# First tile's attention scores as float32 products of two heads, in the upper and lower halves of the array's rows

## The chip, the cores and the metric

One core of one Trainium2 chip runs the whole program. The metric is the device time of the execution in microseconds (us); lower is better. Before: median 653.32 us of three runs (653.1 to 655.28).

## What is computed

Attention with a top-32 mask over 2 batches, 8 heads, 576 tokens and 64 elements a head, then two feed-forward blocks over the 1152 token rows (512 to 2048 to 512, each with its own activation). All in float32.

```python
scores = scale * np.matmul(q, k.transpose(0, 1, 3, 2))
kth = np.partition(scores, -top_k, axis=-1)[..., -top_k:-top_k + 1]      # top_k = 32
scores = np.where(scores >= kth, scores, -1000000000.0)
attn = exp(scores - max); attn = attn / (sum(attn) + 1e-09)
x = np.matmul(attn, v)                            # rows: 2 x 576, columns: 8 heads x 64
h = x @ w_in;  x = (h * np.tanh(softplus(h))) @ w_out       # block 1
h = x @ w_in2; out = (h * sigmoid(h)) @ w_out2              # block 2
```

## The kernel before

**Tiles.** The 1152 rows are nine tiles of 128 (index `t`), the eight heads four pairs (index `p`). `attention(t, p, rank)` does one tile and one pair: scores into two PSUM buffers `ps_att`, copied to `sc` in halves of 288 keys; four rounds of MAX8 (`m8`) and three of MATCH_REPLACE (`rest`) per head on VectorE find the 32nd largest; exponent (`e`) and mask; nine transposes (L439), the copy `pt`, the product with the values into `ps_misc` (L455, L457), and the product with the turned 1/sum into `xt` (L480). Feed-forward block 1 takes tiles in groups 0; 1; 2; 3,4; 5,6; 7,8, block 2 in groups 0,1; 2; 3,4; 5,6; 7,8.

**Scores.** A key tile comes from HBM as `kraw`, with the 64 rows of each head's keys doubled to 128. It is split: a cast to float32r gives the high part (`kk`, all 128 rows), and a subtraction in the lower 64 rows the low part, so one column of `kk` holds high over low. Queries are split in the same manner into two `qs`, high and low, each doubled over the rows. Two float32r products of 128 rows (L378) then give one head's scores against 288 keys. `load_kv` loads and splits the keys once per batch and pair; tiles 0 to 3 and most of tile 4 use batch 0.

**Buffers.** `kraw` has one buffer, `kk` five, `qraw` and `qs` two each, `wide` (weights as loaded) three, `wraw` (weights in float32) nine.

**Weights.** Weights come from HBM in 8-byte elements, and `convert` turns each of 64 pieces of 128x512 into float32: three steps on ScalarE (L505 twice, L517) and two on GpSimd (L509, L519). Block 1's first group uses the pieces of `w1i` as they come, head pair by head pair (L722).

**Order.** The program is listed by `Plan`. Each step has a rank (a start for its tile from `TILES`, plus a time per pair, or a due time from `DUE1`, `DUE2`), a boost from `OFF` that is taken off the rank, and for each engine that can do it an offset from `FLEX` or `FLEX1`. `emit` goes through modelled time; on each engine the step that can start soonest comes next, and of those that can start at once the one with the lowest rank less boost. Buffers of one kind are given out in the order of their users' ranks (L130, L151 to L156). On the chip each engine and the queue of loads on SP (SyncE) run their list strictly in order.

Of the kernel before, what the change touches and what calls it, by code (L numbers as in the profile page):

```python
# [20 lines left out]
P = 128  # L21
# [7 lines left out]
BLOCK1 = [([0], 'n'), ([1], 'n'), ([2], 'n'), ([3, 4], 'r'), ([5, 6], 'r'), ([7, 8], 'r')]  # L29
BLOCK2 = [([0, 1], 'n'), ([2], 'n'), ([3, 4], 'r'), ([5, 6], 'r'), ([7, 8], 'r')]  # L30

TILES = [(19.37, 6.76), (46.36, 14.1), (106.73, 4.63), (204.37, 9.99), (225.06, 11.69), (258.55, 49.85), (345.98,
         18.22), (519.3, 17.23), (461.45, 16.83)]
DUE1 = [(55.53, 32.57), (72.6, 11.18), (185.18, 33.6), (264.74, 3.6), (326.98, 167.36), (749.26, 11.24)]
DUE2 = [(194.98, 61.15), (262.2, 26.21), (504.62, 78.52), (783.18, 203.62), (946.46, 197.95)]

SBUF_BUFS = dict(kraw=1, kk=5, v=5, qraw=2, qs=2, sc=4, rest=1, e=1, pt=2, m8=10, bias=10, den=8, x=3, dt=2, xt=1,
                 wraw=9, ws=8, hs=2, th=1, wide=3, y=2, o=2)
PSUM_BUFS = dict(att=2, misc=1, h=3, y=2)

FLEX = dict(khi=-199.43, klo=-179.86, qhi=-300.0, qlo=65.82, whi=259.95, wlo=-153.31, ghi=-62.92, glo=163.54,
            hs=286.73, mk=-58.0, se=-300.0, den=105.07, y=271.68, sc=-47.47, pt=57.06, dt=-238.16, xlo=98.83)
FLEX1 = dict(khi=245.84, klo=30.36, qhi=-26.57, qlo=179.72, whi=-172.94, wlo=-208.13, ghi=-191.1, glo=300.0, hs=19.48,
             mk=8.23, se=None, den=-282.09, y=None, sc=252.9, pt=None, dt=239.76, xlo=-232.84)
EARLY = 553.02

OFF = dict(kload=578.07, qload=135.46, k=16.71, q=-13.88, sp=314.62, sc=197.87, bias=39.06, e=246.77, tp=342.92,
           pt=330.03, av=-14.23, x=487.41, den=300.22, dw=35.2, dp=222.21, xt=191.17, m=-75.12, cload=96.71,
           cpn=-97.42, cse=5.37, cw=-99.8, cmid=-37.21, wload=572.6, wsplit=-171.63, wstore=206.7, g=-82.77, hs=-40.2,
           y=-31.25, th=709.1)  # L50

PEEK = 0.05

PORT = 0.34
ADD = 1

HBM = 4
# [13 lines left out]
class Plan:  # L71
# [173 lines left out]
def kernel(ctx: ExitStack, tc, qh, kh, va, w1i, w1o, w2i, w2o, out):  # L245
    nc = tc.nc
    NT, DM = out.shape
    NPAIR, D = qh.shape[1], qh.shape[2] // 2
    S = kh.shape[4]
# [4 lines left out]
    SH = S // 2  # L254
    NB = 2 * NM + 1
# [17 lines left out]
    def get(key, make):  # L273
        if key not in T:
            T[key] = make()
        return T[key]

    def copy_ways(n, get_out, get_in, act=0.0, dve=None, twice=False, psum=False):

        ways = []  # L280
        if act is not None:
            ways.append(("act", act_us(n, psum), act, lambda: nc.scalar.copy(get_out(), get_in())))  # L282
        if dve is not None:
            ways.append(("dve", (dve2_us if twice else dve_us)(n), dve, lambda: nc.vector.tensor_copy(get_out(), get_in()), twice))  # L284
        return ways
# [20 lines left out]
    def load_kv(b, p, rank):  # L306
        if (b, p) in kv_done:
            return
        kv_done.add((b, p))
        kk, vv = ("kk", b, p), ("v", b, p)  # L310
        raw = ("kraw", b, p)
        first = b == 0 and p == 0
        for h in ([0], [1]) if first else ([0, 1],):
            hs = slice(h[0], h[-1] + 1)
            add([("sp", 0.06, 0, lambda hs=hs: nc.sync.dma_start(
                out=get(raw, lambda: sbuf("kraw", [P, 2, S]))[:, hs], in_=kh[b, p][:, hs]))],
                writes=[raw + (i,) for i in h], uses=[(raw, "kraw")], rank=rank - 8, boost="kload", load=len(h) * P * S * 4)
        for h in range(2):
            hi = lambda h=h: get(kk, lambda: sbuf("kk", [P, 2, S], F32R))[:, h]
            lo = lambda h=h: T[kk][D:, h]  # L320
            src = lambda h=h: T[raw][:, h]
            U = [(raw, "kraw"), (kk, "kk")]
            add(copy_ways(S, hi, src, dve="khi", twice=True), reads=[raw + (h,)], writes=[kk + (h, 0)], uses=U,
                rank=rank - 6, boost="k")
            add(tt_ways(S, lo, lambda h=h: T[raw][D:, h], lo, ALU.subtract, dve="klo"), reads=[raw + (h,), kk + (h, 0)], writes=[kk + (h, 1)],
                uses=U, rank=rank - 6, boost="k")
        add([("sp", 0.06, 0, lambda: nc.sync.dma_start(out=get(vv, lambda: sbuf("v", [P, NB + 1, D])), in_=va[b, p]))],
            writes=[vv], uses=[(vv, "v")], rank=rank, load=P * (NB + 1) * D * 4)

    def parts(t):  # L330
        r, res = 0, []
# [11 lines left out]
    def attention(t, p, rank):  # L343
        g, j = group_of[t]
# [3 lines left out]
        pp = parts(t)  # L348
        key = (t, p)
        for b, _, _ in pp:  # L350
            load_kv(b, p, rank)
        K = lambda name, *rest: (name,) + key + rest

        add([("sp", 0.06, 0, lambda: nc.sync.dma_start(out=get(K("qraw"), lambda: sbuf("qraw", [P, 2, P])), in_=qh[t, p]))],
            writes=[K("qraw")], uses=[(K("qraw"), "qraw")], rank=rank - 8, boost="qload", load=P * P * 8)
        for i, (b, r0, r1) in enumerate(pp):
            q = K("qs", i)
            mk = lambda x=slice(0, 2), q=q: get(q, lambda: sbuf("qs", [P, 2, 2, P], F32R))[:, x]
            if len(pp) > 1:
                add([("pool", 0.6, 0, lambda mk=mk: nc.gpsimd.memset(mk().bitcast(F32), 0.0))], writes=[q], uses=[(q, "qs")],  # L360
                    rank=rank - 6)
            raw = lambda r0=r0, r1=r1: T[K("qraw")][:, :, r0:r1]
            hi, lo = (lambda x=x, mk=mk, r0=r0, r1=r1: mk(x)[:, :, r0:r1] for x in range(2))
            U = [(q, "qs"), (K("qraw"), "qraw")]
            add(copy_ways(2 * (r1 - r0), hi, raw, dve="qhi", twice=True), reads=[K("qraw")], writes=[q], uses=U,
                rank=rank - 6, boost="q")
            add(tt_ways(2 * (r1 - r0), lo, raw, hi, ALU.subtract, dve="qlo"), reads=[K("qraw"), q], writes=[q], uses=U,
                rank=rank - 6, boost="q")
        sc = lambda: get(K("sc"), lambda: sbuf("sc", [P, 2, S]))
        for h in range(2):  # L370
            for f in range(2):
# [60 lines left out]
        for c in range(0, NB, 3):  # L432
            tp = K("tp", c)
# [448 lines left out]
```

## Time and profile before

| | |
|---|---|
| median of three runs | 653.32 us |
| profiled execution | 655.83 us, span 654.1 us |
| TensorE busy | 606.1 us (93%) |
| VectorE busy | 539.5 us (82%) |
| ScalarE busy | 476.3 us (73%) |
| GpSimd busy | 382.3 us (58%) |
| mean granted TensorE clock | 0.987 |
| HBM traffic | 271 GB/s over the span |

The profile is of one execution. A share of busy time is a mean over stages with different bounds, so the table of stretches and the chain of waits say more. PE is TensorE's products, PEld its weight loads, DVE is VectorE, ACT ScalarE, POOL GpSimd, SP the queue of loads. L and a number is a line of the kernel before. Casts, copies and subtractions of all kinds share the helper lines L282, L284, L290 and L292; the names of their tiles tell them apart.

### The profile page before, as it was taken

What the parts mean: (1) busy time and instruction counts of PE and PEld (TensorE: products, weight loads), DVE (VectorE), ACT (ScalarE), POOL (GpSimd) and SP (SyncE); (2) the same over time, 40 slices, a digit from 0 to 9 for tenths busy, and PEclk for the clock granted to TensorE, in tenths of its full rate; (3) what the DMA queues carried; (4) which work ended last, traced back from release to release, by engine and by line L of the source; (5) the groups of instructions that cost most, each with busy time, mean ns of one, the idle gap of its engine ahead of it and who ended that gap; (6) DMA issues with size and microseconds to landing.
All of it is one profiled execution on the core that took longest, in us unless ns stands there. A gap on an engine that the chain in (4) does not pass through costs nothing.

```text
span 654.1 us, 13089 instructions
## 1 busy us (share of the span) xinstructions
PE 606.1 (93%) x4536; PEld 537.0 (82%) x4536; DVE 539.5 (82%) x1106; ACT 476.3 (73%) x993; POOL 382.3 (58%) x334
## 2 busy tenths in 40 slices
PE   1298788999999999999999999999999999999997
PEld 1177667999999866668999878999988899999996
DVE  4999999997999999989999979979998234554550
ACT  6799999988699998988978666878777344332321
POOL 6898569761267888987549236556787233322221
PEclk9999967999999999999999999999999999999999
DMA  8987649898789868799999589875876998887752
GB/s 309 293 256 222 197 159 330 312 361 263 204 271 345 276 192 271 268 305 347 389 402 368 151 272 355 316 259 191 272 255 223 374 300 294 278 263 256 246 179 80
DMA packets 85650, 178.34 MB, mean 273 GB/s; under 512 B 8144, under 2 KB 29136, under 8 KB 85584
## 3 DMA queue, kind: packets, MB, share of 16 engines
q1 hardware_dynamic: 85584, 177.50, 80.4%
q8 instruction: 36, 0.59, 0.3%
q14 instruction: 30, 0.25, 0.1%
HBM read 138.94 MB, written 38.54 MB: 271 GB/s over the span
## 4 chain that ended last, share of the span: by engine, by line
PE 53%; DVE 16%; ACT 15%; DMA 7%; issue 4%; POOL 4%; SPq 1%; POOLq 0%; ACTq 0%
PE ps_h L630 20%; PE ps_y L701 12%; PE ps_y L808 11%; DVE m L394 6%; DVE rest L397 5%; ACT ws L505 4%; PE ps_att L378 3%; DMA wraw<-w1i 3%; PE ps_att L439 2%; PE ps_misc L455 2%; ACT wraw L517 2%; ACT pt L282 2%; ACT e L410 2%; DVE e L414 2%; POOL wraw L519 2%
## 5 line engine op out<-in xcount | busy, mean ns | idle before, releaser
L394 DVE MAX8 m<-rest 128x8 f32<-128x576 f32 x216 | 154.4, 745 | 0.1
L397 DVE MATCH_REPLACE8 rest<-m,rest 128x576 f32<-128x576 f32 x144 | 106.2, 741 | 0.0
L509 POOL TENSOR_TENSOR ws<-ws 128x512 int32<-128x512 int32 x64 | 86.7, 1359 | 28.9 <-ACT ws L505 27.2
L378 PE MATMUL ps_att<-kk,qs 128*128 128x288 f32 x320 | 72.8, 346 | 31.6 <-POOL kk L290 24.5
L282 ACT CAST ws<-wraw 128x512 fp32r<-128x512 f32 x93 | 57.4, 621 | 53.8 <-PE ps_h L630 25.3
L519 POOL TENSOR_TENSOR wraw<-wraw,ws 128x512 int32<-128x512 int32 x64 | 85.5, 1346 | 15.9 <-ACT wraw L517 11.0
L505 ACT ACTIVATE ws<-wide,zone 128x512 int32<-128x512 int16 x128 | 94.5, 779 | 0.0
L378 PEld LDWEIGHTS ps_att<-kk,qs 128*128 128x128 f32 x320 | 51.3, 205 | 43.2 <-POOL kk L290 26.0
L292 DVE TENSOR_TENSOR ws<-wraw,ws 128x512 fp32r<-128x512 f32 x65 | 58.9, 924 | 31.3 <-ACT ws L282 30.9
L630 PE MATMUL ps_h<-y,ws 128*128 128x256 f32 x576 | 75.3, 280 | 0.0
L630 PEld LDWEIGHTS ps_h<-y,ws 128*128 128x128 f32 x576 | 73.1, 188 | 2.7
L290 POOL TENSOR_TENSOR ws<-wraw,ws 128x512 fp32r<-128x512 f32 x44 | 57.6, 1318 | 27.3 <-ACT ws L282 14.8
L630 PE MATMUL ps_h<-xt,ws 128*128 128x256 f32 x576 | 72.8, 282 | 0.0
L701 PE MATMUL ps_y<-wide,ws 128*128 128x256 f32 x540 | 71.3, 283 | 0.0
L630 PEld LDWEIGHTS ps_h<-xt,ws 128*128 128x128 f32 x576 | 69.5, 188 | 1.5 <-issue 1.2
L290 POOL TENSOR_TENSOR wide<-th,wide 128x512 fp32r<-128x512 f32 x24 | 31.5, 1313 | 66.7 <-DVE wide L284 65.4
L701 PEld LDWEIGHTS ps_y<-wide,ws 128*128 128x128 f32 x540 | 66.5, 189 | 0.0
L808 PE MATMUL ps_y<-ws,wide 128*128 128x512 f32 x252 | 64.8, 396 | 0.0
L290 POOL TENSOR_TENSOR wide<-hs,wide 128x512 fp32r<-128x512 f32 x24 | 32.0, 1342 | 49.4 <-DVE wide L284 40.2
L439 PE MATMUL ps_att<-ident,e 128*128 128x128 f32 x324 | 52.6, 287 | 6.7 <-DVE e L414 3.9
L701 PE MATMUL ps_y<-hs,wraw 128*128 128x128 f32 x384 | 52.4, 286 | 2.2 <-ACT hs L670 2.2
L394 DVE MAX8 m<-sc 128x8 f32<-128x576 f32 x72 | 52.8, 747 | 1.3 <-ACT sc L282 0.7
(89 smaller groups left out, 1231.5 us busy)
## 6 DMA issues: line engine op xcount, KB each, us to landing
wraw<-w1i SPq DMA_DIRECT2D x64, 256.0 KB, 4.8
wraw<-w2i SPq DMA_DIRECT2D x64, 256.0 KB, 4.0
ws<-w1o_split SPq DMA_DIRECT2D x30, 512.0 KB, 5.1
ws<-w2o_split SPq DMA_DIRECT2D x28, 512.0 KB, 4.4
wraw<-w1o SPq DMA_DIRECT2D x48, 256.0 KB, 5.8
wide<-in_w1i_dram SPq DMA_DIRECT2D x16, 512.0 KB, 5.6
wide<-in_w1o_dram SPq DMA_DIRECT2D x16, 512.0 KB, 5.0
wide<-in_w2i_dram SPq DMA_DIRECT2D x16, 512.0 KB, 5.1
```

What stands on the lines that cost most here:

```text
L282: ways.append(("act", act_us(n, psum), act, lambda: nc.scalar.copy(get_out(), get_in())))
L290: ways.append(("pool", pool_us(n), pool, lambda: nc.gpsimd.tensor_tensor(out=get_out(), in0=get_a(), in1=get_b(), op=op)))
L378: nc.tensor.matmul(o, lhsT=l, rhs=r[:, f * SH:(f + 1) * SH], start=(i == 0), stop=(i == len(ops) - 1))
L394: add([("dve", 0.67, 0, lambda i=i, h=h, src=src: nc.vector.max(out=m8()[:, h, 8 * i:8 * i + 8], in_=src()[:, h]))], reads=srck, writes=[K ...
L397: add([("dve", 0.73, 0, lambda i=i, h=h, src=src: nc.vector.match_replace(out=rest()[:, h], in_to_replace=m8()[:, h, 8 * i:8 * i + 8], in_ ...
L439: nc.tensor.transpose(o[:, i, :], ef[:, (c + i) * P:(c + i + 1) * P], ident)
L505: add([("act", act_us(UNIT) + 0.14, 0, lambda i=i: nc.scalar.activation(pn()[:, i], top(), AF.Relu, scale=ONE16 - 2 * ONE16 * i, bias=zone))],
L509: ways = [("pool", pool_us(UNIT), 0, lambda: nc.gpsimd.tensor_tensor(out=se(), in0=pn()[:, 0], in1=pn()[:, 1], op=ALU.subtract))]
L519: add([("pool", pool_us(UNIT), 0, lambda: nc.gpsimd.tensor_tensor(out=w().bitcast(I32), in0=w().bitcast(I32), in1=se(), op=ALU.add))], rea ...
L630: nc.tensor.matmul(hp[:, c, :], lhsT=l, rhs=rr, start=(i == 0), stop=(i == len(ops) - 1))
L701: nc.tensor.matmul(yp[:, o, :], lhsT=l[:, d * P:(d + 1) * P], rhs=rr[:, c, :], start=(fc == 0 and k == 0 and o == 0), stop=last, skip_grou ...
L808: nc.tensor.matmul(op, lhsT=gg[:, c, i * P:(i + 1) * P], rhs=wt, start=(fc == 0 and k == 0), stop=(fc == NFC - 1 and k == len(ops) - 1))
```

## The change

Tile 0 (`PLAIN = (0,)`) takes keys and queries as they are, without a split. Head 0 is in the upper 64 rows, head 1 in the lower 64, and each half of the keys is one step of two float32 products into two PSUM buffers. The keys' split becomes a function of its own, `split_k`, which is first called by tile 1. Raw and split keys share six buffers of `kk`. All tables of ranks, boosts and offsets have new values.

```diff
-SBUF_BUFS = dict(kraw=1, kk=5, v=5, ...
+SBUF_BUFS = dict(kk=6, v=5, ...
-TILES = [(19.37, 6.76), (46.36, 14.1), (106.73, 4.63), (204.37, 9.99), ...
+TILES = [(28.06, 7.53), (50.67, 14.47), (106.31, 7.12), (204.4, 8.97), ...
-DUE1 = [(55.53, 32.57), (72.6, 11.18), (185.18, 33.6), ...
+DUE1 = [(56.14, 34.7), (72.58, 21.42), (181.07, 37.87), ...
-OFF = dict(kload=578.07, qload=135.46, k=16.71, ... cload=96.71, ...
+OFF = dict(kload=608.39, qload=87.44, k=22.76, ... cload=-16.98, ...
+PLAIN = (0,)
 def load_kv(b, p, rank):
-                out=get(raw, lambda: sbuf("kraw", [P, 2, S]))[:, hs], in_=kh[b, p][:, hs]))],
-                writes=[raw + (i,) for i in h], uses=[(raw, "kraw")], rank=rank - 8, boost="kload", ...
+                out=get(raw, lambda: sbuf("kk", [P, 2, S]))[:, hs], in_=kh[b, p][:, hs]))],
+                writes=[raw + (i,) for i in h], uses=[(raw, "kk")], rank=rank - 8, boost="kload", ...
+def split_k(b, p, rank):          # once per (b, p); the casts and subtractions that stood in load_kv
...
-            U = [(raw, "kraw"), (kk, "kk")]
+            U = [(raw, "kk"), (kk, "kk")]
 def attention(t, p, rank):
             load_kv(b, p, rank)
+            if t not in PLAIN:
+                split_k(b, p, rank)
-        for i, (b, r0, r1) in enumerate(pp):
+        for i, (b, r0, r1) in enumerate(pp if t not in PLAIN else ()):       # query splits
+        for f in range(2) if t in PLAIN else ():
+            sp = [K("sp", h, f) for h in range(2)]
+            def plain(f=f, sp=sp):
+                for h in range(2):
+                    rows = slice(h * D, h * D + D)
+                    nc.tensor.matmul(get(sp[h], lambda: psum("att", [P, SH])), lhsT=T[K("qraw")][rows, h],
+                                     rhs=T["kraw", b, p][rows, h, f * SH:(f + 1) * SH], start=True, stop=True)
+            add([("pe", 0.8, 0, plain)], reads=[K("qraw"), ("kraw", b, p, 0), ("kraw", b, p, 1)], writes=sp, ...
+            for h in range(2):
+                add(copy_ways(SH, lambda h=h, f=f: sc()[:, h, f * SH:(f + 1) * SH], lambda x=sp[h]: T[x], ...
-        for h in range(2):
+        for h in range(2) if t not in PLAIN else ():
             for f in range(2):
                 sp = K("sp", h, f)
```

## Rows read from the trace of the kernel before

**Rows 1.** Stretches: length; PE, PEld, DVE, ACT, POOL busy us; granted clock; DMA share, GB/s
```profile
9.00:60.00 51.00, 29.65 (x171) 24.33 (x172) 50.02 (x105) 45.82 (x94) 43.86 (x36) 1.00 0.90 286
70.00:80.00 10.00, 8.78 (x71) 7.16 (x69) 9.80 (x23) 10.00 (x26) 4.86 (x5) 1.00 0.66 197
80.00:90.00 10.00, 7.36 (x37) 6.10 (x38) 9.72 (x23) 9.97 (x18) 5.26 (x5) 0.58 0.39 113
90.00:100.00 10.00, 7.31 (x43) 6.20 (x43) 10.00 (x23) 9.99 (x22) 6.43 (x7) 0.84 0.59 211
100.00:110.00 10.00, 8.24 (x52) 7.52 (x53) 9.45 (x19) 9.44 (x20) 9.34 (x8) 0.72 0.96 307
110.00:654.00 544.00, 534.47 (x4086) 476.88 (x4084) 440.17 (x896) 377.78 (x792) 298.51 (x259) 1.00 0.81 278
```
**Rows 2.** Chain of waits, 0 to 60 us, then 60 to 104: shares, pieces
```profile
by line: DVE m L394 30.5%; DVE rest L397 23.6%; DMA wide<-in_w1i_dram 10.7%; DVE e L414 8.0%; issue 4.5%; PE ps_h L722 3.4%; ACT ws L505 3.2%; ACT wraw L517 3.2%; ACT pt L282 1.9%; DVE qs L284 1.5%; SPq L354 1.4%; SPq L315 1.3%; ACT e L410 
...
30.42 1.46 DVE rest L397 x2
31.87 1.32 DVE m L394 x2
...
by line: ACT ws L505 26.3%; ACT wraw L517 11.4%; ACT e L410 9.9%; issue 9.1%; ACT pt L282 8.8%; ACT sc L282 7.7%; POOL wraw L519 5.8%; ACT hs L670 4.6%; ACT hs L282 4.3%; POOL ws L509 3.3%; ACT L410 2.9%; ACT dt L282 2.2%; ACT qs L282 2.1%;
```
**Rows 3.** Waits of TensorE, whole span: us in total, times, longest us
```profile
PE ps_att L378 <- POOL kk L290: 24.5, 3, 9.8
```
**Rows 4.** SP queue at the start (start us, us), and stretches of 2 us
```profile
0.72 0.86 SPq L315 DMA_DIRECT2D kraw<-in_kh_dram  x2
1.63 0.90 SPq L354 DMA_DIRECT2D qraw<-in_qh_dram  x2
...
2.00:4.00 2.00, 0.00 (x0) 0.00 (x0) 0.00 (x0) 0.40 (x1) 0.00 (x0) 1.00 0.89 315
6.00:8.00 2.00, 0.47 (x1) 0.14 (x1) 0.00 (x0) 0.40 (x1) 1.92 (x3) 1.00 1.06 358
```
**Rows 5.** Instructions in order of time: start us, us, what, idle time before it
```profile
3.60 1.48 ACT L282 CAST kk<-kraw 128x576 fp32r<-128x576 f32 x2 [1.60 <-DMA kraw<-in_kh_dram]
4.98 0.40 ACT L282 CAST qs<-qraw 128x256 fp32r<-128x256 f32 x1
9.01 0.67 ACT L517 ACTIVATE wraw<-wide 128x512 int32<-128x512 uint32 x1 [2.27 <-DMA wide<-in_w1i_dram]
9.64 0.76 DVE L394 MAX8 m<-sc 128x8 f32<-128x576 f32 x1
31.86 2.73 PE L378 MATMUL ps_att<-kk,qs 128*128 128x288 f32 x8 [8.83 <-POOL kk L290]
34.66 2.81 PE L439 MATMUL ps_att<-ident,e 128*128 128x128 f32 x9
69.20 0.29 DVE L480 TENSOR_TENSOR xt<-ps_misc,dt 128x128 f32<-128x128 f32 x1
```
**Rows 6.** The same view: float32 products at full and half width
```profile
41.41 2.07 PE L722 MATMUL ps_h<-xt,wraw 128*128 128x128 f32 x8 [0.68 <-DVE xt L480]
51.88 1.09 PE L455 MATMUL ps_misc<-pt,v 128*64 128x128 f32 x16
55.42 1.05 PE L722 MATMUL ps_h<-xt,wraw 128*128 128x128 f32 x8
```
**Rows 7.** Groups by line, 0 to 60 us: busy us, mean ns, idle before
```profile
L517 ACT ACTIVATE wraw<-wide 128x512 int32<-128x512 uint32 x15 | 10.1, 676 | 3.6 <-DMA wide<-in_w1i_dram 3.2 <-PE ps_att L439 0.4
L282 ACT CAST qs<-qraw 128x256 fp32r<-128x256 f32 x6 | 2.4, 404 | 1.0 <-DMA qraw<-in_qh_dram 1.0
L290 POOL TENSOR_TENSOR kk<-kraw,kk 64x576 fp32r<-64x576 f32 x8 | 11.6, 1474 | 3.3 <-DMA kraw<-in_kh_dram 3.1
L284 DVE COPY sc<-ps_att 128x288 f32<-128x288 f32 x5 | 2.3, 452 | 8.8 <-PE ps_att L378 8.7
```
**Rows 8.** Waits of TensorE's weight loads, whole span: us in total, times, longest
```profile
PEld ps_misc L455 <- issue: 5.8, 20, 0.8
```

More of the change, by code (lines that the diff above doesn't have):

```diff
@@ L30 @@
 BLOCK2 = [([0, 1], 'n'), ([2], 'n'), ([3, 4], 'r'), ([5, 6], 'r'), ([7, 8], 'r')]
[L32 to L37, printed above, removed]
+TILES = [(28.06, 7.53), (50.67, 14.47), (106.31, 7.12), (204.4, 8.97), (228.13, 9.44), (251.93, 48.93), (339.09,
+         14.84), (544.45, 15.95), (508.61, 11.93)]
@@ L38 @@
+DUE1 = [(56.14, 34.7), (72.58, 21.42), (181.07, 37.87), (264.49, 3.4), (328.08, 127.63), (770.05, 10.76)]
+DUE2 = [(194.96, 63.53), (262.66, 22.33), (489.18, 97.29), (836.89, 208.21), (1017.87, 176.37)]
+SBUF_BUFS = dict(kk=6, v=5, qraw=2, qs=2, sc=4, rest=1, e=1, pt=2, m8=10, bias=10, den=8, x=3, dt=2, xt=1,
                  wraw=9, ws=8, hs=2, th=1, wide=3, y=2, o=2)
 PSUM_BUFS = dict(att=2, misc=1, h=3, y=2)
-FLEX = dict(khi=-199.43, klo=-179.86, qhi=-300.0, qlo=65.82, whi=259.95, wlo=-153.31, ghi=-62.92, glo=163.54,
-            hs=286.73, mk=-58.0, se=-300.0, den=105.07, y=271.68, sc=-47.47, pt=57.06, dt=-238.16, xlo=98.83)
@@ L43 @@
[L43 to L50, printed above, removed]
@@ L52 @@
-PEEK = 0.05
-PORT = 0.34
+FLEX = dict(khi=160.94, klo=-131.85, qhi=-300.0, qlo=-121.8, whi=201.94, wlo=-32.46, ghi=-264.27, glo=-258.34,
+            hs=174.88, mk=151.77, se=-140.65, den=-80.51, y=300.0, sc=-145.93, pt=59.31, dt=-5.98, xlo=175.24)
+FLEX1 = dict(khi=141.86, klo=136.65, qhi=-26.45, qlo=133.59, whi=145.08, wlo=-291.44, ghi=-103.6, glo=-11.08,
+             hs=38.75, mk=39.78, se=None, den=-118.72, y=None, sc=296.41, pt=None, dt=300.0, xlo=-49.66)
+EARLY = 559.36
+OFF = dict(kload=608.39, qload=87.44, k=22.76, q=-16.29, sp=238.91, sc=165.63, bias=127.91, e=228.22, tp=367.53,
+           pt=451.83, av=14.38, x=624.87, den=370.98, dw=96.55, dp=228.54, xt=170.88, m=-115.49, cload=-16.98,
+           cpn=-115.59, cse=25.73, cw=-53.73, cmid=-26.87, wload=612.68, wsplit=-319.71, wstore=228.61, g=-104.3,
+           hs=-21.89, y=26.54, th=732.7)
@@ L55 @@
+PEEK = 0.03
+PORT = 0.21
 ADD = 1
@@ L315, in load_kv @@
             add([("sp", 0.06, 0, lambda hs=hs: nc.sync.dma_start(
-                out=get(raw, lambda: sbuf("kraw", [P, 2, S]))[:, hs], in_=kh[b, p][:, hs]))],
-                writes=[raw + (i,) for i in h], uses=[(raw, "kraw")], rank=rank - 8, boost="kload", load=len(h) * P * S * 4)
+                out=get(raw, lambda: sbuf("kk", [P, 2, S]))[:, hs], in_=kh[b, p][:, hs]))],
+                writes=[raw + (i,) for i in h], uses=[(raw, "kk")], rank=rank - 8, boost="kload", load=len(h) * P * S * 4)
+        add([("sp", 0.06, 0, lambda: nc.sync.dma_start(out=get(vv, lambda: sbuf("v", [P, NB + 1, D])), in_=va[b, p]))],
+            writes=[vv], uses=[(vv, "v")], rank=rank, load=P * (NB + 1) * D * 4)
+    kk_done = set()
+    def split_k(b, p, rank):
+        if (b, p) in kk_done:
+            return
+        kk_done.add((b, p))
+        kk, raw = ("kk", b, p), ("kraw", b, p)
         for h in range(2):
@@ L326, in load_kv @@
                 uses=U, rank=rank - 6, boost="k")
-        add([("sp", 0.06, 0, lambda: nc.sync.dma_start(out=get(vv, lambda: sbuf("v", [P, NB + 1, D])), in_=va[b, p]))],
-            writes=[vv], uses=[(vv, "v")], rank=rank, load=P * (NB + 1) * D * 4)
     def parts(t):
@@ L369, in attention @@
         sc = lambda: get(K("sc"), lambda: sbuf("sc", [P, 2, S]))
-        for h in range(2):
+        for f in range(2) if t in PLAIN else ():
[5 more added lines that the diff above has]
+                                     rhs=T["kraw", b, p][rows, h, f * SH:(f + 1) * SH], start=True, stop=True)
+            (b, _, _), = pp
+            add([("pe", 0.8, 0, plain)], reads=[K("qraw"), ("kraw", b, p, 0), ("kraw", b, p, 1)], writes=sp, rank=rank - 10,
+                boost="sp", uses=[(x, "ps_att") for x in sp] + [(K("qraw"), "qraw"), (("kraw", b, p), "kk")])
+            for h in range(2):
+                add(copy_ways(SH, lambda h=h, f=f: sc()[:, h, f * SH:(f + 1) * SH], lambda x=sp[h]: T[x], dve="sc", psum=True),
+                    reads=[sp[h]], writes=[K("sc", h, f)], uses=[(sp[h], "ps_att"), (K("sc"), "sc")], rank=rank - 10, boost="sc")
+        for h in range(2) if t not in PLAIN else ():
             for f in range(2):
```

## Prediction

> **What bounds the kernel now.** I read the table of stretches first. From 110 us to the end TensorE is busy 534.5 of 544.0 us, so there only its work and the moment at which it is fully supplied count; ahead of that it is not the bound [rows 1]. The chain of waits says what is: up to 60 us over half of it is VectorE's top-32 search (MAX8 30.5%, MATCH_REPLACE 23.6%), and from 60 to 104 us it is ScalarE, mostly turning weights into float32 (26.3% and 11.4%) [rows 2]. The reader should see in the table that both are full there: ScalarE has 5.2 us idle between 9 and 60 us and none from 70 to 80, VectorE 1.0 us and 0.2. In 70 to 110 us TensorE loses time in two ways: 8.3 us idle, and a granted clock of 0.58, 0.84 and 0.72 (1.00 is the 2.4 GHz level, 0.50 the 1.2 GHz level) in three stretches, which on 7.36, 7.31 and 8.24 us of work is 3.1 + 1.2 + 2.3 = 6.6 us. Together 14.9 us that an earlier supply could give back [rows 1]. Last come the waits of TensorE's queue: 24.5 us, in three waits, for GpSimd's key splits [rows 3]. That is the stall which the change takes away. TensorE has little else to do early, but its queue is in order: the third pair's scores wait 8.8 us and start at 31.86 us, and the transposes of pair 0 stand behind them, at 34.66 [rows 5].
>
> **The change, part by part.** All sums are against the profiled execution, 655.83 us (span 654.1 and 1.7 around it), which lies 2.5 above the median of 653.32; differences carry over to the median.
>
> *Order of the loads.* Raw keys had one buffer; now they share six with the split ones, and nothing holds them at the start. SP takes its steps by rank less boost. For keys that is 28.06 - 8 - 608.39 = -588 for pair 0, and -566 for pair 3; for the first queries 28.06 - 8 - 87.44 = -67; for the first weights 16.1 - 10 + 17.0 = +23. So all four pairs' keys (288 + 288 + 3 x 576 KB) now go ahead of the first queries, where before only pair 0's did [rows 4]. Three more transfers of 576 KB are 1.77 MB, at 0.36 MB per us (358 GB/s in a full stretch [rows 4]) 4.9 us. To the first queries there are 2.49 MB: counted from 2.0 us that is 6.9 us, and 0.7 us go from the last byte to use (pair 0's first half, 0.29 MB, counted in the same way at 315 GB/s, is there at 2.9 us, and its cast starts at 3.60 [rows 4, 5]): usable at 9.6 us against 4.98 before [rows 5]. The same 4.9 us go on the first weights, used at 9.01 us before [rows 5]. SP issues seven transfers in 3.2 us at 0.45 each, so the issue itself is no bound.
>
> *The products.* A float32 product is two records. Eight records of 128 columns take 2.07 us early and 1.05 us later [rows 6]; for 288 columns, and two heads (four records), that is 2.3 or 1.2 us one after the other. No row shows two halves of rows side by side. The nearest are the value products, which use two halves of the columns: 16 records in 1.09 us, where 8 at full width take 1.05, a ratio of 0.52 [rows 6]. From the two ends, side by side (0.52) and in turn (1.0), I take the first: 1.2 us at the early pace. There are two PSUM buffers, so the second half of the keys waits until the first is copied (0.45 us [rows 7]). First search with both heads at hand: 9.6 + 1.2 + 0.45 + 1.2 + 0.45 = 12.9 us. Before, VectorE searched without gap from 12.48 us and had 1.6 us of it done by then (MAX8 at 9.64, one replacement [rows 5]): an effective start of 10.9. Loss +2.0; in turn it is 2 x 1.1 more, of which the first head's lead hides about 1, so +3.2. In sum TensorE spends 8 x 1.2 = 10 us on these scores against 4 x 2.73 = 11 before [rows 5], where it has 21 of 51 us free [rows 1]: nothing.
>
> *A rule that speaks against it.* TensorE's weight loads of the value products, the first to use half the columns after full-width work, start 0.29 us late (5.8 us in 20), put down to nothing but issue [rows 8]. The Trainium skill (TensorEngine Tiling, Key Properties) says that changing the tiling mode drains TensorE, which agrees with that row; the row halves of this change would pay it too. By it two changes stand before the first search, about 0.6 us, and the sum below would end 0.6 later; without it, as below.
>
> *Splits removed and moved.* Tile 0's query splits go: one on VectorE (1.5% of 60 us on the chain, 0.9 [rows 2]), the others on ScalarE at 0.40 each [rows 7], of which I count one behind 9 us. VectorE's side: +2.0 - 0.9 = +1.1. The key splits (0.74 a head on ScalarE [rows 5], 1.47 on GpSimd [rows 7]) aren't removed: tile 1 needs them. Pair 0's casts, which lay in ScalarE's empty first 9 us, now come behind. ScalarE: +4.9 + 1.5 - 0.4, less what it fills of its 5.2 us idle: between +0.8 and +6.0. Of the idle 3.2 us are waits for these weights [rows 7]; since the later key loads leave the queue I take them as filled, with 0.8 us of the other waits: +2.0. The two engines run beside each other: the worse counts, +2.0. GpSimd is given 11.6 us of room [rows 7], and has 5 us idle in each of the stretches from 70 to 90 us [rows 1], which hide its later splits; without that cover 2 x 1.47 us a pair would show.
>
> *What the freed queue gives.* With no product of tile 0 waiting for a split, pair 0's transposes follow its mask, and pair 3's scores can be ready at any time. Tile 0's fourth and last x lands at 69.20 us [rows 5]. VectorE needs per pair about 8 x 0.66 + 6 x 0.73 + 1.6 + 0.6 = 11.9 us (two searches 1.32, two replacements 1.46, the mask 8.0% of 60 us in three pairs [rows 2], and 0.6 for the small ones), 47 for the tile, of the 56.7 between 12.48 and 69.20: some 9 us of it went to tile 1. Tile 0's last x can come between 0 and 9 us earlier. I take half, 4.5: the first block's hidden layer ends that much sooner, and out of the 14.9 us lost in 70 to 110 so much comes back. What is late next is ScalarE's conversion of w1o, since it is full at 70 to 100 us [rows 1].
>
> *Ranks.* They move every later step; the profile can't show the new order. TensorE's idle time behind 110 us is 9.5 us, so little can be gained there; a worse order could open gaps as well. I take zero, with -3 and +3 as bounds, a third of that idle time.
>
> **Sum:** +2.0 - 4.5 = -2.5, so 653.3 for such an execution and 650.8 for the median. Bounds of the terms: +0.8 - 9 = -8.2 and +6.0 - 0 = +6.0; with ranks 642 to 662.
>
> **The rivals.**
> 1. *ScalarE keeps the gain.* It is full from 70 to 100 us whatever arrives; an earlier x of tile 0 then only makes its conversions the wait. For: nothing of its work there goes. Against: its 5.2 us idle earlier can take some. The -4.5 shrinks to about -2: 653.3.
> 2. *The keys in front decide (slower).* Place: the SP queue's first seven loads. Price: the 4.9 us of three key transfers on weights and queries. It decides if ScalarE can't fill its gaps and tile 0's order stays as it was: then +3 to +6 reach TensorE's full stretch, which has 9.5 us in 544 to take them back. For: VectorE is at 98% from 9 us on, ScalarE at 90% and from 70 us at 100% [rows 1]. Against: VectorE's own loss is only 1.1. Middle +4: 657.3.
> 3. *The heads don't run side by side.* The change then isn't what it says; the start is 1.2 later, 652.0.
> 4. *The new order gains behind 110 us too:* 3 more on top of a gain of 4, 646.
>
> **How the numbers follow.** Chances: forecast 0.38 (own range 648 to 651.3), first rival 0.20, second 0.32, third 0.05, fourth 0.05. A measurement of this kernel tells 0.3%, 2.0 us, from no change: faster is below 651.4, slower above 655.3. Faster: 0.38 + 0.05 = 0.43; same 0.20 + 0.05 = 0.25; slower 0.32. The range that leaves out 2 in 10: 643 to 660.
>
> **What would show it.** Right: the first MAX8 at about 12 to 13 us (9.64 before), the first weights used near 14; no wait of TensorE's scores for a GpSimd key split before 46 us; tile 0's fourth x before 66 us; stretches 80 to 110 with a granted clock nearer 1. The pair of heads: starts of upper and lower rows a few tens of ns apart for side by side. Wrong: the full stretch of TensorE starting after 110 us (rival 2), or ScalarE full and x early but nothing gained (rival 1). A first MAX8 before 10 us would say that the queue of loads was misread.

## The result and the profile after

The changed kernel takes 661.89 us in the median of four runs (660.86 to 663.78); the kernel before took 653.49 in four beside it. The ratio is 1.0126, 95% interval 1.0094 to 1.0159: slower by 8.4 us, where 2.5 us faster was forecast, and outside the range. The profiled execution after took 660.86 us (span 658.0), the one before 655.83 (span 654.1). So the two traces hold 5.0 us of the 8.4, 3.9 of them in the span: the execution traced before was one of the longer ones (the spans of its 91 runs beside the experiments have a median of 652.4), the one after the shortest of four.

The stretches of the changed kernel, with the columns of [rows 1]:

```profile
9.00:60.00 51.00, 35.54 (x208) 25.22 (x209) 45.38 (x98) 45.16 (x98) 41.02 (x32) 0.97 0.85 269
60.00:70.00 10.00, 4.97 (x29) 4.17 (x27) 10.00 (x20) 8.68 (x17) 9.69 (x8) 0.76 0.79 246
70.00:80.00 10.00, 8.51 (x42) 6.67 (x41) 10.00 (x23) 9.21 (x21) 7.53 (x8) 0.50 0.74 239
80.00:90.00 10.00, 7.40 (x57) 6.90 (x56) 8.97 (x20) 8.91 (x19) 6.38 (x6) 0.84 0.70 220
90.00:100.00 10.00, 7.63 (x52) 6.74 (x51) 9.73 (x24) 9.96 (x18) 5.95 (x6) 0.70 0.53 173
100.00:110.00 10.00, 8.43 (x75) 7.38 (x73) 9.96 (x23) 10.00 (x24) 7.33 (x7) 1.00 0.78 240
110.00:658.00 548.00, 535.99 (x4088) 477.17 (x4087) 445.79 (x921) 379.50 (x795) 268.95 (x238) 1.00 0.80 276
```

The reader should see two things. TensorE did more between 9 and 60 us than before (35.5 us against 29.7 [rows 1]), as the change means it to. VectorE did less: 45.4 us against 50.0, and it is this third busy column that most of the rest is about. The prediction counted 14.9 us of TensorE's time lost from 70 to 110 us, part of which was to come back. The same sum from these rows is 8.0 us idle and 7.7 for the granted clock (0.50, 0.84, 0.70 and 1.00 on 8.51, 7.40, 7.63 and 8.43 us of work), 15.8 in all: none of it came back.

The same view for VectorE alone, over 0 to 110 us and from there to the end of its last MAX8; first the kernel before, then the changed one:

```profile
0.00:110.00 110.00, 99.32 (x211) 0.92 0.78 247
110.00:503.30 393.30, 375.21 (x802) 1.00 0.84 287
```
```profile
0.00:110.00 110.00, 94.05 (x203) 0.88 0.78 247
110.00:506.80 396.80, 376.92 (x802) 1.00 0.83 285
```

And single instructions of the changed kernel (start us, us, what, idle time before it), which answer to [rows 4, 5]: loads, first products, first weights, first search; then tile 0's fourth x, what TensorE waited for ahead of it, and two key splits.

```profile
0.72 2.29 SPq L317 DMA_DIRECT2D kk<-in_kh_dram  x5
3.05 1.15 SPq L367 DMA_DIRECT2D qraw<-in_qh_dram  x2
4.24 4.54 SPq L526 DMA_DIRECT2D wide<-in_w1i_dram  x3
11.76 1.33 PE L389 MATMUL ps_att<-kk,qraw 64*128 64x288 f32 x4 [11.76 <-DMA qraw<-in_qh_dram]
13.53 0.66 ACT L544 ACTIVATE wraw<-wide 128x512 int32<-128x512 uint32 x1
15.64 1.41 DVE L421 MAX8 m<-sc 128x8 f32<-128x576 f32 x2
9.08 2.75 POOL L292 TENSOR_TENSOR kk<-kk 64x576 fp32r<-64x576 f32 x2 [1.92 <-ACT kk L284]
23.77 2.80 POOL L292 TENSOR_TENSOR kk<-kk 64x576 fp32r<-64x576 f32 x2
66.02 2.08 PE L749 MATMUL ps_y<-xt,wraw 128*128 128x128 f32 x8 [4.45 <-POOL wraw L546]
76.87 0.28 DVE L507 TENSOR_TENSOR xt<-ps_misc,dt 128x128 f32<-128x128 f32 x1
```

The first search starts at 15.64 us, 6.0 later than before. TensorE's 24.5 us of waits for key splits [rows 3] are gone from its list, but it is idle for 37.5 of the first 110 us, where it was idle for 38.4 before. The waits have other names now; these are the longest:

```profile
PE ps_att L389 <- DMA qraw<-in_qh_dram: 11.8, 1, 11.8
PE ps_att L466 <- DVE e L441: 8.2, 11, 2.6
PE ps_att L466 <- ACT sc L284: 5.2, 5, 3.3
```

**A distance that stays the same.** The last MAX8, VectorE's last search, ends at 503.3 us before and at 506.8 after; the span ends 150.8 and 151.3 us behind it. In the fifteen traces of the changed kernel and of the experiments below that distance is 150.6 to 151.5 us, while the end itself moves over 17.6 us. (In the rows below a MAX8 that starts at 519.13 us and takes 0.75 is such a last search.) So what makes one version slower than another lies ahead of the last search. The distance doesn't say which engine it is, for two of them are nearly full up to there. All engines from 320 to 503 us, before and after:

```profile
320.00:503.00 183.00, 181.87 (x1466) 165.00 (x1465) 173.97 (x372) 137.80 (x315) 111.64 (x96) 1.00 0.82 283
320.00:503.00 183.00, 182.16 (x1480) 165.99 (x1479) 171.90 (x367) 141.19 (x316) 113.72 (x96) 1.00 0.83 291
```

TensorE is idle for 1.1 and 0.8 us there, VectorE for 9.0 and 11.1. In all sixteen traces TensorE loses at most 1.1 us from 320 us to the last search, so the versions part earlier. The table gives VectorE's idle time and work up to its last search, which add up to where that search ends, and TensorE's idle time from 110 us to the end of the span:

| kernel | VectorE idle 0 to 110 | VectorE idle behind 110 | VectorE work | last MAX8 ends | span | TensorE idle behind 110 |
|---|---|---|---|---|---|---|
| before | 10.7 | 18.1 | 474.5 | 503.3 | 654.1 | 9.6 |
| after | 16.0 | 19.9 | 471.0 | 506.8 | 658.0 | 12.0 |
| late start | 14.7 | 18.7 | 473.8 | 507.2 | 657.7 | 11.2 |
| twice the products | 12.3 | 16.9 | 474.2 | 503.3 | 653.9 | 9.8 |
| more work for VectorE | 9.7 | 17.3 | 480.0 | 507.0 | 657.8 | 10.9 |
| den ahead | 13.5 | 19.8 | 472.7 | 506.0 | 657.4 | 13.2 |
| late splits | 17.2 | 21.6 | 471.8 | 510.6 | 661.9 | 13.8 |
| copies on ScalarE | 10.5 | 19.3 | 473.9 | 503.7 | 654.5 | 10.4 |
| relief | 10.7 | 18.1 | 473.6 | 502.3 | 653.1 | 9.9 |
| old products, new order | 27.0 | 20.0 | 472.9 | 519.9 | 671.0 | 13.5 |
| the same, early queries | 20.2 | 20.2 | 472.6 | 512.9 | 664.2 | 13.5 |

VectorE's columns are read as the two pairs above: length less busy. Each row is one execution, and executions of one kernel lie 2 to 6 us apart (653.10 to 655.28 before), so smaller differences between rows show nothing by themselves. Idle time and work add up to the end for any engine; the sum alone names no cause.

Two things can be read. The change gives VectorE 5.3 us more idle time ahead of 110 us and 1.8 behind, and takes 3.5 us of work off it. That work is not just tile 0's: up to the last search VectorE even has six score copies more than before (25 against 19), and the new tables give other steps to other engines, among them nine casts of weights (2 against 11) and five subtractions for split x (9 against 14). And the last column parts the two orders. In the eight traces with the changed kernel's order it is 12.0 to 13.8 us, in the eight with the order before 9.5 to 11.4; the means are 2.8 us apart, and the gaps lie between 110 and 320 us.

### The profile page after: what moved, and what is told of

Read it like the earlier page. It is cut to its first block, busy times and chain, and to the rows that moved or that the text cites. A ratio compares the mean times of both kernels' runs of the same rounds, so it can differ in the third digit from the quotient of the medians.

```text
span 658.0 us, 13060 instructions
## 1 busy us (share of the span) xinstructions
PE 608.5 (92%) x4536; PEld 534.2 (81%) x4536; DVE 539.8 (82%) x1123; ACT 474.7 (72%) x989; POOL 350.3 (53%) x311
## 4 chain that ended last, share of the span: by engine, by line
PE 56%; DVE 29%; ACT 10%; DMA 2%; issue 2%; SPq 0%; DVEq 0%; ACTq 0%
PE ps_h L657 23%; DVE m L421 12%; PE ps_y L835 11%; PE ps_y L728 10%; DVE rest L424 10%; DVE e L441 4%; PE ps_misc L482 3%; ACT ws L532 3%; PE ps_att L405 3%; PE ps_att L466 2%; ACT sc L284 1%; DMA qraw<-in_qh_dram 1%; PE ps_misc L484 1%; ACT pt L284 1%; ACT wraw L544 1%
## 5 line engine op out<-in xcount | busy, mean ns | idle before, releaser
L284 ACT CAST ws<-wraw 128x512 fp32r<-128x512 f32 x101 | 61.1, 621 | 51.1 <-PE ps_h L657 26.8
L546 POOL TENSOR_TENSOR wraw<-wraw,ws 128x512 int32<-128x512 int32 x64 | 83.8, 1324 | 7.6 <-ACT wraw L544 6.5
L292 POOL TENSOR_TENSOR ws<-wraw,ws 128x512 fp32r<-128x512 f32 x49 | 64.0, 1327 | 16.7 <-ACT ws L284 12.3
L294 DVE TENSOR_TENSOR ws<-wraw,ws 128x512 fp32r<-128x512 f32 x60 | 45.2, 758 | 30.9 <-ACT ws L284 30.6
L466 PE MATMUL ps_att<-ident,e 128*128 128x128 f32 x324 | 55.1, 295 | 14.9 <-DVE e L441 8.2
L405 PE MATMUL ps_att<-kk,qs 128*128 128x288 f32 x288 | 61.3, 329 | 3.0 <-ACT sc L284 1.6
L466 PEld LDWEIGHTS ps_att<-ident,e 128*128 128x128 f32 x324 | 39.7, 149 | 27.4 <-issue 9.6
L284 ACT COPY pt<-ps_att 128x384 f32<-128x384 f32 x107 | 47.7, 479 | 7.5 <-PE ps_att L466 7.1
L424 DVE MATCH_REPLACE8 rest<-m,sc 128x576 f32<-128x576 f32 x72 | 53.1, 740 | 0.0
```

The source lines that it names most:

```text
L292: ways.append(("pool", pool_us(n), pool, lambda: nc.gpsimd.tensor_tensor(out=get_out(), in0=get_a(), in1=get_b(), op=op)))
L405: nc.tensor.matmul(o, lhsT=l, rhs=r[:, f * SH:(f + 1) * SH], start=(i == 0), stop=(i == len(ops) - 1))
L424: add([("dve", 0.73, 0, lambda i=i, h=h, src=src: nc.vector.match_replace(out=rest()[:, h], in_to_replace=m8()[:, h, 8 * i:8 * i + 8], in_ ...
L466: nc.tensor.transpose(o[:, i, :], ef[:, (c + i) * P:(c + i + 1) * P], ident)
L546: add([("pool", pool_us(UNIT), 0, lambda: nc.gpsimd.tensor_tensor(out=w().bitcast(I32), in0=w().bitcast(I32), in1=se(), op=ALU.add))], rea ...
```

## The experiments

Theories: T, the prediction's own, by which TensorE's early waits are worth time; A, the late start; B, the new form of the products costs by itself; C, the new order costs; D, formed after the first seven runs, that VectorE's chain sets the end and all else counts by what it does to that. Ratios are to the kernel before, run on the same chip; they compare means, so a difference of two medians can be 1 us off them. Where an order is edited, all other steps keep engine and place.

**Queries first**, in the changed kernel's order:

```diff
-SP: keys of pairs 0, 1, 2, 3; queries of pairs 0, 1; w1i
+SP: keys of pair 0; queries of pairs 0, 1; keys of pairs 1, 2, 3; w1i
-ScalarE, GpSimd: key splits of pair 1 ahead of the first score copy
+ScalarE, GpSimd: key splits of pair 1 behind it
```


> The changed kernel with its order of steps kept, except that the first two query loads go ahead of the keys of pairs 1 to 3, and pair 1's key splits go behind the first copy of scores. Theory A, the late queries: VectorE's search starts near 9 us instead of 15.6, and since VectorE is full to 140 us the total falls by 3 to 5 us from 661.9, to 657 to 659. Theory B, the late weights: they land as late as in the changed kernel, so the total stays within 1.5 us of 661.9. Theory C, the new order of the later steps: nothing at the start matters, within 1.5 us too.

Measured: 660.01 us, ratio 1.0078 (1.0055 to 1.0100). The first search starts at 10.4 us in place of 15.6, and only 1.9 us of the 8.4 come back by the medians, 3.1 by the ratios (the intervals of the two just overlap): VectorE then waits 4.2 us for two `den` steps that stand in ScalarE's queue behind conversions. The time lies between A's 657 to 659 and the 660.4 or more of B and C.

**Start as before**: in addition the first three `w1i` loads ahead of the keys of pairs 1 to 3, and pair 1's splits behind the first conversion.

```diff
-SP: ...; keys of pairs 1, 2, 3; w1i, three loads
+SP: ...; w1i, three loads; keys of pairs 1, 2, 3
```


> The same, with the first three weight loads too ahead of the keys of pairs 1 to 3, so that the first loads go in the order of the kernel before. Theory A: like the run with the queries first, 657 to 659. Theory B: weights 4.5 us earlier, ScalarE and GpSimd convert them earlier, and the total falls by 4 us or more more than with the queries alone, to 653 to 657. Theory C: within 1.5 us of 661.9.

Measured: 661.14 us, 1.0090 (1.0065 to 1.0115). Weights are used from 8.6 us on, and nothing is gained by it, as C said.

**Late start**: the kernel before, with three more loads of 576 KB ahead of its first queries.

```diff
 keys of pair 0, second half: nc.sync.dma_start(out=kraw, in_=kh[b, p])
+for i in range(3): nc.sync.dma_start(out=unused, in_=kh[0, i + 1])
```


> The kernel before, in its own order, with three more loads of 576 KB (keys of pairs 1 to 3, into buffers that are not yet in use, read by nobody) ahead of its first queries and weights. Theories A and B: the start is as late as in the changed kernel, queries near 11 us and weights near 13, and 4 to 8 us of it reach the end: 657 to 661. Theory C: the later order is that of the kernel before and takes the delay up in its gaps, below 655.

Measured: 658.40 us, 1.0059 (1.0037 to 1.0082). The first search starts at 13.95 us, 4.3 later, and the end of the trace comes 3.6 later. In the old order a late start is passed on nearly whole, as A and B said.

**Same rows**: the changed kernel with both heads in the upper 64 rows (keys and queries lie in both halves, so the scores are the same).

```diff
-rows = slice(h * D, h * D + D)
+rows = slice(0, D)
```


> The changed kernel with both heads' products in the upper 64 rows of the array (the keys and queries lie in both halves, so the result is the same), nothing else moved. If heads in two halves of the rows run side by side, four records take about 2.3 us early instead of 1.33, VectorE starts 1 to 2 us later, and the total rises by 1 to 2 us. If they don't, nothing changes, within 1 us.

Measured: 664.97 us, 1.0164 (1.0135 to 1.0194). TensorE's products of two pairs, in the changed kernel and here:

```profile
35.00 0.76 PE L389 MATMUL ps_att<-kk,qraw 64*128 64x288 f32 x4
38.23 0.76 PE L389 MATMUL ps_att<-kk,qraw 64*128 64x288 f32 x4
```
```profile
35.22 1.24 PE L389 MATMUL ps_att<-kk,qraw 64*128 64x288 f32 x4
38.42 1.23 PE L389 MATMUL ps_att<-kk,qraw 64*128 64x288 f32 x4
```

Two heads in two halves of the rows take 0.76 us, in one half 1.24 (granted clock 1.00 in both): they do run side by side, at 0.61 of the time. Read one by one, the records of the two heads start 0.006 or 0.007 us apart at 35.00 and again at 35.35 in the changed kernel; here the four start at 35.22, 35.57, 35.81 and 36.05. The total is 3.1 us above the changed kernel's, but the two intervals overlap.

**Old order**: the new products in the order of the kernel before.

```diff
-tile 0: query splits; eight steps of split products, one copy behind each
+tile 0: per half of the keys one step of two plain products, a copy on VectorE and one on ScalarE
-SP: queries of four later pairs where they stood
+SP: each behind the plain products that free its buffer
```


> The new products of tile 0 (float32, two heads in the two halves of the rows, key tile shared) in the order of emission of the kernel before: the twelve split products and query splits of tile 0 are left out, the eight plain products stand where each pair's first split product stood, and four query loads go behind the plain products that free their buffers. Every other step keeps its engine and its place. Theory C (the new order costs, the product form does not): the wait for key splits (24.5 us of TensorE's idle time by 42 us, rows 3) goes, the end follows by at most a few us: 648 to 654, not slower than before. Theory B (the new form itself costs, by row halves, by keys held longer or by copies): slower than before, 656 to 662, near the changed kernel.

Measured: 658.39 us, 1.0048 (1.0032 to 1.0064): 3 us slower than before, with no wait for a key split left. That is B's range, and C's forecast (not slower) fails. TensorE's waits did not go, they changed their names, and it is idle for 40.4 of the first 110 us:

```profile
PE ps_att L507 <- DMA qraw<-in_qh_dram: 6.1, 1, 6.1
PE ps_att L507 <- DMA kk<-in_kh_dram: 5.8, 1, 5.8
PE ps_att L507 <- ACT sc L402: 5.4, 3, 4.2
PE ps_att L507 <- DVE rest L542: 4.7, 1, 4.7
```

VectorE had eight score copies here in place of five, and 1.4 us waits for the second half of the keys, since both PSUM buffers are taken by the first.

**Old products**: the mirror, split products and query splits at the plain ones' places in the changed kernel's order.

> The mirror: the split products and query splits of tile 0 as before, put at the places of the plain ones in the order of emission of the changed kernel; its loads, ranks, conversions and shared key buffers are kept. Theory C: the order decides, so 660 to 666, as slow as the changed kernel or slower by the 2 to 4 us that the splits cost in the first 40 us. Theory B: the product form decides, so near before: 652 to 657.

Measured: 674.57 us, 1.0303 (1.0275 to 1.0331), which neither theory gave. The first row is of TensorE's waits up to 60 us, the second VectorE's last search:

```profile
PE ps_att L524 <- ACT qs L403: 21.0, 3, 12.0
...
519.13 0.75 DVE L540 MAX8 m<-rest 128x8 f32<-128x576 f32 x1
```

The edit had put the query casts where they held TensorE up for 21 us, so the run measured itself more than the order. It is repeated better below.

**Late splits**: queries first, and each key split behind the conversions that stand ahead of its first reader.

```diff
-ScalarE, GpSimd: key splits of pairs 0 to 3 within the first 27 us; batch 1's pair 0 from 57 us
+ScalarE, GpSimd: each shortly before tile 1's scores of the pair; batch 1's pair 0 near its old place
```


> The changed kernel with the queries ahead of the keys of pairs 1 to 3 (as in the run queries first), and with every key split moved behind the weight conversions that stand ahead of its first reader: pairs 0 to 3 shortly before tile 1's scores of that pair, batch 1's pair 0 near the place it had before. Nothing else moves. If the early splits are what holds the first MLP layer back (they stand ahead of the conversions for which TensorE waited 4.4 us at 61.6 us in the changed kernel): the fourth x of tile 0 and the first h come earlier, 654 to 657. If not, 659 to 661 as the run with queries first (660.0).

Measured: 663.63 us, 1.0124 (1.0098 to 1.0149), a miss: slower than queries first, not faster. VectorE's waits up to 110 us:

```profile
DVE sc L296 <- PE ps_att L399: 8.2, 2, 6.8
DVE den L503 <- ACT den L499: 5.0, 3, 4.3
DVE m L431 <- ACT sc L294: 2.0, 1, 2.0
```

With conversions in the splits' place, ScalarE's small steps for the search stand behind conversions that wait for their loads. So no gain from later splits was found, though the edit brought waits of its own. These seven traces laid beside each other gave D; the next two runs test it on the kernel before.

**Twice the products**:

```diff
-for i, (l, r) in enumerate(ops):
+for i, (l, r) in list(enumerate(ops)) * (2 if t == 0 and p > 0 else 1):
```


> The kernel before with the split products of tile 0's pairs 1 to 3 issued twice into the same tiles, which adds about 8 us of TensorE work in the first 42 us (three times 2.73, rows 5) and makes the scores of three pairs 2.7 us later. Theory D (VectorE's chain of MAX8 and MATCH_REPLACE8 is what the first 110 us wait for, and it runs with hardly a gap behind 12.5 us; TensorE's waits for key splits lie beside it): no change, 653 to 656. Theory T, the prediction's own (TensorE's waits on the way to the first scores are on the path): 657 to 663.

Measured: 656.00 us, 1.0018 (1.0005 to 1.0032). TensorE's products of pairs 1 and 2 (before: 20.31 and 31.86, 2.73 us each), and VectorE's last search:

```profile
20.81 3.67 PE L378 MATMUL ps_att<-kk,qs 128*128 128x288 f32 x16 [10.20 <-POOL kk L290]
33.01 4.21 PE L378 MATMUL ps_att<-kk,qs 128*128 128x288 f32 x16 [8.53 <-POOL kk L290]
...
502.52 0.76 DVE L394 MAX8 m<-rest 128x8 f32<-128x576 f32 x1
```

The edit added less than meant, since the longer blocks ran faster (0.23 and 0.26 us a product, not 0.34): the scores are complete 1.4 and 2.6 us later. By the ratio the time rises by 1.2 us (0.3 to 2.1), and VectorE is idle for 1.6 us more ahead of 110 us. The last search ends where it did in the trace before, which was one of the longer executions. Both waits for key splits are still there, 18.7 us long.

**More work for VectorE**:

```diff
-nc.vector.max(out=m8[...], in_=src)
+[nc.vector.max(out=m8[...], in_=src) for _ in range(2 if t == 0 and p == 1 else 1)]
```


> The kernel before with the eight MAX8 of tile 0's second pair done twice, which adds 8 x 0.67 = 5.3 us of VectorE work at 24 to 36 us and nothing to any other engine. Theory D: the end moves by most of it, 658 to 660. Theory T: VectorE has room in the stretch in which TensorE waits, 654 to 656.

Measured: 661.18 us, 1.0108 (1.0083 to 1.0133): 7.1 us (5.4 to 8.7) for 5.3 us of work. The last search, in the shortest of the six runs (659.59 us):

```profile
506.27 0.76 DVE L394 MAX8 m<-rest 128x8 f32<-128x576 f32 x1
```

The second run is clear: T forecast 654 to 656 for it, and VectorE's early work is paid in full. The first fits D, but with half the delay that was meant it is weaker evidence against T: products that come up to 2.6 us later cost 1.2, about what VectorE's idle time grew by. Both edits lie ahead of 42 us, so they say nothing of what sets the pace behind 110.

**Den ahead**: queries first, and ScalarE's `den` of tile 0's pairs 0 and 1 ahead of the conversions that VectorE had waited behind.

```diff
-ScalarE: ws, ws, den (pair 0), ...; sc, sc, qs, den (pair 1)
+ScalarE: den (pair 0), ..., ws, ws; den (pair 1), sc, sc, qs
```


> The changed kernel with the queries first (660.0 us) and, besides, ScalarE's two small den steps of tile 0's first two pairs ahead of the conversions and casts behind which VectorE waited 2.3 and 1.9 us for them. Everything else of the new order stays, the w1i conversions become 1.4 us later. Theory D: VectorE gets back some 4 us of its first 110, so 655 to 657. Theory C (the new order of conversions and splits costs by itself): no better than 660, up to 662.

Measured: 660.62 us, 1.0085 (1.0066 to 1.0105): no gain, a miss for D's number. VectorE, stretches and waits up to 110 us:

```profile
0.00:110.00 110.00, 96.50 (x206) 0.92 0.79 251
110.00:506.00 396.00, 376.17 (x798) 1.00 0.83 285
```
```profile
DVE sc L296 <- PE ps_att L399: 9.4, 3, 6.6
DVE xt L517 <- PE ps_misc L494: 1.9, 2, 1.1
DVE den L503 <- ACT den L499: 1.2, 2, 0.9
```

The 3 us taken from `den` came back as other waits but for 1.3 us. The distance to the end stays (506.0 + 151.4), but D's estimate of what one wait is worth fails: behind it stands the next.

**Copies on ScalarE**: the old order with the new products, VectorE relieved.

```diff
-pairs 1 to 3: of four score copies two on VectorE
+pairs 1 to 3: all four on ScalarE
+pair 0: ScalarE's copies ahead of its first conversions
```


> The new products in the old order again (658.4), with VectorE relieved: the score copies of pairs 1 to 3 all on ScalarE (VectorE does two copies in place of eight, 6 x 0.45 = 2.7 us less), and pair 0's copies ahead of ScalarE's first weight conversions, so that no copy waits behind them. Theory D: 2.5 to 5 us less than that run, 652 to 656, at or under the kernel before. Theory B (the new form costs by itself): 657 to 659.

Measured: 656.31 us, 1.0029 (1.0017 to 1.0041), by the ratios 1.2 us less than the old order with eight copies (2.1 by the medians; the intervals overlap), still 1.9 above the kernel before, and between D's range and B's. VectorE starts at 8.52 us and has as little idle time ahead of 110 us as before. Where its lead goes is seen at 300 us:

```profile
302.40 0.62 ACT L402 CAST ws<-wraw 128x512 fp32r<-128x512 f32 x1 [3.14 <-DMA wraw<-w1i]
302.93 0.39 ACT L402 COPY sc<-ps_att 128x288 f32<-128x288 f32 x1
```
```profile
303.35 0.76 DVE L539 MAX8 m<-sc 128x8 f32<-128x576 f32 x1 [2.04 <-ACT sc L402]
```

ScalarE waits 3.1 us for a weight load, a score copy stands behind it, and VectorE waits 2.0 us for the copy.

**Copy ahead**: the last kernel with that copy ahead of the waiting split, and `den` ahead of conversions. The recorded text speaks of the first pair's `den`; the edit moves that of all four pairs of tile 0.

```diff
-ScalarE: ws (w1i, waits for its load); sc (tile 6, pair 0)
+ScalarE: sc (tile 6, pair 0); ws (w1i, waits for its load)
-ScalarE: conversions (w1i); den (tile 0, each pair)
+ScalarE: den (tile 0, each pair); conversions (w1i)
```


> The last run (new products, old order, copies on ScalarE, 656.3 us) with two steps of ScalarE's queue exchanged with their neighbours: the score copy of tile 6's first pair ahead of the split of a w1i chunk that waited 3.1 us for its DMA at 299 us (VectorE waited 2.0 us there for that copy), and den of tile 0's first pair ahead of one weight conversion (VectorE waited 1.1 us at 22.6 us). Theory D (each us of VectorE's waits before its last MAX8 moves the end): 1.5 to 2.5 us less, 653.5 to 655, level with the kernel before. If VectorE's waits are not what is left there: 656 as before.

Measured: 657.82 us, 1.0050 (1.0033 to 1.0068), a miss: the 2.0 us wait is gone, 1.7 us of others stand near it, and ahead of 110 us VectorE is busy 1.1 us less.

**Relief**: the kernel before, with two score copies and a query cast of tile 0 on ScalarE.

```diff
-VectorE: sc (pair 1), sc (pair 2), qs (pair 2)
+ScalarE: sc (pair 1), sc (pair 2), qs (pair 2)
```


> The kernel before, in its own order, with three VectorE steps of tile 0 given to ScalarE at the same place: one score copy each of pairs 1 and 2 (0.45 us) and the query cast of pair 2 (0.88 us), together 1.8 us less VectorE work before 36 us. Theory D: the end comes earlier by up to that, 652 to 653.5 (ratio 0.997 to 0.999), less what waits for ScalarE take back. Theory T: no change, 654 to 655.

Measured: 654.93 us, 1.0004 (0.9990 to 1.0018): no change; the 1.8 us that D allowed at most lie outside the interval. Added VectorE work is paid in full, work taken away gives nothing that can be measured, so D as it was put (all counts by VectorE's chain) is not borne out. Why is not settled. The wait at 300 us in the run with the copies on ScalarE, for a load that comes no earlier, is one place where a lead can end; TensorE, nearly full from 110 us on, is a rival that no run tests.

**Old products, early queries**: the second mirror.

```diff
-ScalarE, GpSimd: query splits directly ahead of their pair's products
+ScalarE, GpSimd: pairs 0 and 1 behind the key splits of pair 1, pairs 2 and 3 well ahead of their products
```


> As the run with the old split products in the changed kernel's order (674.6 us), but with tile 0's query splits early in place of directly ahead of their products: pairs 0 and 1 behind the key splits of pair 1, pairs 2 and 3 two thirds of the way from their loads to their products. In that run TensorE waited 21.0 us for ScalarE's query casts, so it told little of the order. Here key and query splits are both ahead of the products, and products, copies, loads and conversions stand in the changed kernel's order. Theory C (the order costs, the product form little): 660 to 665. If the product form is worth much in this order: 666 or more. If the new form itself is what costs: 655 to 658.

Measured: 665.86 us, 1.0200 (1.0170 to 1.0231). TensorE still waited 15.7 us for query casts, 12.3 of them at the very start, where the changed kernel waits 11.8 for the loads. So in the new order the old form is slower than the new one, with those waits in it, and the old order with the old form faster than all. For the old form the order's cost can't be told from the waits. With the new form it is the step from 1.0029 (copies on ScalarE) to 1.0126, 0.0097 of 654 us or 6.3, of which queries first gave 1.9 to 3.1 back.

No version beat the kernel before.

## Why the prediction was wrong

- **What bounds it, and what the freed queue gives.** The chain and the table were read rightly for VectorE (98% busy between 9 and 60 us [rows 1, 2]), and then TensorE's 24.5 us of waits [rows 3] were called the stall that the change takes away, and its going the source of the term -4.5. That step failed. VectorE had hardly any room for earlier scores, and TensorE's waits passed to loads, copies and VectorE's own steps: idle 38.4 of the first 110 us before, 37.5 after, 40.4 with the new products in the old order. Tile 0's fourth x was to come 4.5 us earlier, before 66 us; it came at 76.87, 7.7 later than [rows 5]. The first three came about 5 us earlier (35.9, 48.9 and 57.8 against 41.1, 53.8 and 61.7): with VectorE full, tiles 0 and 1 shared it otherwise. At 66.02 TensorE had waited 4.45 us for a weight converted late. The new products in the old order were 3 us slower, not faster.
- **Behind 110 us** only TensorE's work and its supply were to count. From 320 us on the rows agree (0.8 to 1.1 us idle to the last search). Between 110 and 320 TensorE is idle for 4.7 us before and 7.5 after.
- **Order of the loads.** Right in kind, too small. The queries were usable at 11.76 us, not at 9.6. The sum counted the keys in front at 358 GB/s; between 4 and 8 us 309 and 293 were reached, and the three weight loads issued behind the queries moved at the same time (by 11 us some 3.0 MB had come, not 2.49). The weights came as said (13.53 against about 14).
- **Start of the search.** Taken as 10.9 to 12.9 us, +2.0; it was 15.64, +4.7. Of the 2.7 us more, 2.2 are the queries, the rest the second half of the products (1.43 us behind the copies). The late start in the old order shows its worth, 3.9 us; in the new order restoring it gave 1.9 to 3.1.
- **The products.** Side by side, as taken: 1.33 us for a block of two heads against 1.2. Rival 3 is out. What the switch of tiling mode costs no run isolates; ahead of the blocks at 35.00 and 38.23 TensorE's weight loads pause for 0.12 us, where [rows 8] has 0.29, and its products not at all.
- **Splits.** "GpSimd is given 11.6 us of room" was false: the new ranks put the key splits of all pairs within the first 27 us (9.08 and 23.77 above), earlier than before. Moving them later did not help, so no cost of this error was found.
- **Ranks** were taken as zero within 3 either way; of the 6.3 us between the best run in the old order and the changed kernel the late start is 1.9 to 3.1, so some 3 to 4 are the rest of the order, and 1.9 are left between the kernel before and that run. This term was too small, and on the side of which the prediction said that a worse order could open gaps: TensorE's idle time behind 110 us is 2.8 us longer on average in the new order's traces. Which steps of the order are to blame stays open: two attempts to mend single waits (den ahead, late splits) moved them on to the next.
- **Rival 2**, keys in front, gave the sign and the place, and 657.3 us for the time. Its mechanism is 2 to 3 us of the loss in the new order, about 4 in the old; that the whole loss was twice its price is the order's part.

## What to carry to other kernels

Before a long list of waits is priced as a stall, look at the engine that takes the results. If it is full, an earlier result only waits there, and the first engine's wait changes its name. An instruction at a fixed distance from the end in several runs tells behind which point they are alike; which engine sets the pace ahead of it is told by every engine's idle time there, and by runs that add work to one. In the order before, a late start and added VectorE work were paid nearly in full, while waits and work taken away gave little or nothing. When a change comes with a new order, run form and order apart before saying which it was, and compare also which engine got which steps.

## What the runs showed of the hardware

VectorE's mask step (L414, L441: two operands in SBUF) takes longer beside GpSimd. In the kernel before, 18 of its 48 instructions overlap no GpSimd instruction and take 0.80 to 0.82 us; the 30 that do overlap one take 0.80 to 1.96, mean 1.16. In the copies-on-ScalarE run, GpSimd's key split and the two masks beside it:

```profile
18.11 3.27 POOL L410 TENSOR_TENSOR kk<-kk 64x576 fp32r<-64x576 f32 x2
```
```profile
18.44 1.68 DVE L559 SCALAR_TENSOR_TENSOR e<-sc,m,e 128x576 f32<-128x576 f32 x1
20.05 1.94 DVE L559 SCALAR_TENSOR_TENSOR e<-sc,m,e 128x576 f32<-128x576 f32 x1
```

The Trainium skill (SBUF — State Buffer, SBUF: two separate sides) says that a VectorE instruction with two SBUF inputs and a GpSimd instruction that reads SBUF lock each other out for a whole instruction. The rows agree: one by one, GpSimd's two steps run from 18.11 to 19.50 and from 19.46 to 21.38 us, the masks from 18.44 to 20.12 and from 20.05 to 22.00, so each step that starts while the other engine's runs ends 0.6 us (a mask) or 1.3 us (GpSimd's) behind the other's end. Over 30 masks it is some 10 us of VectorE's time, more than the change was about; no run tried to take it away, so what it would give is not shown.
